# Turning a layer's results on VectorE and through DRAM instead of on TensorE

## The chip, the core and the metric

The kernel runs on one core of a Trainium2 chip. A core has five engines with instruction queues of their own: TensorE (PE, matrix products), VectorE (DVE), ScalarE (ACT), GpSimd (POOL) and SyncE (SP, which here only issues transfers). Each takes its instructions in order, and an instruction that waits holds up all those behind it. Transfers run on the core's 16 DMA engines; they are put on them by SyncE, ScalarE and GpSimd. Matrix products are written to PSUM, everything else works in SBUF.

The metric is the device time of one execution in microseconds, from the first instruction to the last, as the median of several runs. Before the change it is 434.11 us (three runs, 433.49 to 434.98).

## The reference

The computation has two parts. The first is linear attention with a decay, in blocks of 64 positions; its output for 4 sequences of 768 positions becomes 3072 rows (tokens) of 512 numbers:

```python
B, H, S, D = attn_out.shape
x = np.ascontiguousarray(attn_out.transpose(0, 2, 1, 3)).reshape(B * S, H * D)
return _moe_ref(x=x, **moe_kwargs)
```

The second part sends each token to one of eight experts by a hash of its id. An expert is two matrix products with a ReLU between them, and the result is written to the token's own row:

```python
expert_idx = token_ids * np.int64(2654435761) % np.int64(E)
for e in range(E):
    mask = expert_idx == e
    xe = x[mask]
    h = np.maximum(xe @ w1[e], 0.0)
    out[mask] = h @ w2[e]
```

w1 is 512 x 1024 and w2 is 1024 x 512 numbers of four bytes, so each is 2 MB per expert.

## The kernel before, in words

**Stages.** From 0 to about 100 us of the profile runs the attention, in 24 units of 128 positions; its results are stored to a tensor x_pieces in DRAM. Meanwhile the routing is computed: which expert has how many tokens, and lists of row numbers. Then come the experts, one at a time, in eight *windows* (ORDER), each with a fixed number of places for tokens (CAPS, 376 to 432). This document is about the windows.

**A window.** A token's row of x is gathered by GpSimd (gather_window, take) in squares of 32 tokens, turned by VectorE (turn_in), and then lies with features on the partitions and tokens along them. Both layers keep this form: layer one makes hT (1024 features) from xT, layer two makes yT (512 features) from hT. Each layer is done with seven products of quarter size instead of eight (function seven), as in Strassen's method. The sums that this needs are made on VectorE: of the weights (weight_sums, L625), of the tokens (token_sums, L637 and L638) and of the products (L667, L686, L687, L689). The first layer runs seven twice, over two halves of its 1024 features (g = 0 and 1), the second once. In seven, `both` makes products 1 and 2, `others` the products 7, 5, 6, 4 and 3, in that order. The list `todo` holds instructions that `others` hands out between the sums: the weight sums of w2 for this window in the first layer, and in the second layer the weight sums of w1 for the next window and the turn of its x.

**Products and PSUM.** Products 1, 2, 6, 4 and 3 go to the pool psA (4 buffers), 7 and 5 to psC (2 buffers). The pool psB (2 buffers) is free in the windows, except for the results' transposes.

**Getting the results out.** The output needs tokens on the partitions. In the window after the one that made them, tiles_out takes yT in tiles of 128 tokens; rows_out turns each on TensorE with four transposes (L725) into a psB buffer, ScalarE (even tiles, L730) or VectorE (odd tiles, L732) copies it to a tile osb, and GpSimd scatters its rows to the output by their numbers (scatter, L736). Tiles 0 and 1 are done after `both` of the first half, the others after `both` of the second half. w2's columns are ordered in advance so that the copy's rearranging gives the right order of features. The last window has no window after it and calls rows_out itself.

**The order of the work.** It is the order of the program, engine by engine (a manual schedule). Where an instruction stands in the loop over windows therefore decides what it stands behind in its engine's queue. After the code of the first layer the loop issues, on SyncE, the next window's w1 (load_window_w1, L113) and then its w2 (load_window_w2, L119); three buffers of 2 MB hold weights, so a load also waits until its buffer is free. Before each, SyncE reads the expert's number into a register (L123, L127).

Of the kernel before, what the change touches and what calls it, by code (L numbers as in the profile page):

```python
# [7 lines left out]
F32 = mybir.dt.float32  # L8
# [11 lines left out]
CAPS = [376, 384, 392, 392, 400, 408, 416, 432]  # L20
# [5 lines left out]
ORDER = [0, 2, 3, 4, 5, 6, 7, 1]  # L26
SQ = 32
# [4 lines left out]
def kernel(  # L32
# [8 lines left out]
    nc = tc.nc  # L41
    P = 128
# [3 lines left out]
    B, NCH, _, _, D = qkv.shape  # L46
    N, _ = out.shape
    E, _, F = moe_w1.shape
# [3 lines left out]
    NB = P // SQ  # L52
# [10 lines left out]
    DP = D // P  # L63
    FP = F // P
    NT = -(-max(CAPS) // P)
# [3 lines left out]
    def pool(name, bufs, c=ctx, **kw):  # L69
        return c.enter_context(tc.tile_pool(name=name, bufs=bufs, **kw))  # L70
# [18 lines left out]


    x_dram = nc.dram_tensor("x_pieces", ((1 + NC) * DP * P, P), F32)

    order = ExitStack()
    order.enter_context(tc.manual_schedule(engines={
# [136 lines left out]
    idx_all = route.tile([P, NTILE], I32)  # L231
# [289 lines left out]
    def gather_window(e):  # L521


        n = -(-CAPS[e] // SQ)
        xT = xin.tile([P, DP, n * SQ], F32, tag="xT", name=f"xT_{e}")

        g = scratch[:, 0:n * P].rearrange("p (b q) -> p b q", q=P) if e == 0 else xin.tile(
            [P, n, P], F32, tag="g", name=f"g_{e}")

        def gather(b):  # L530
            rows = (1 + (EARLY if e == 0 and b < FIRST // SQ else NC)) * DP * P
            t, k = divmod(b, NB)
            take(g[:, b, :], x_rows[:, e * NT + t, k:k + 1], rows)

        return xT, [lambda b=b: gather(b) for b in range(n)], lambda b0, b1: turn_in(xT, g, b0, b1)
# [68 lines left out]
    mwork = pool("mwork", 2)  # L604
# [12 lines left out]
    def weight_sums(w, name, keep=False):  # L617
        K, M = w.shape[1] // 2, w.shape[2] // 2
        b = [[w[:, j * K:(j + 1) * K, k * M:(k + 1) * M] for k in range(2)] for j in range(2)]
        t = sums.tile([P, 3, K, M], F32, tag=f"t{M}", name=f"{name}_t")  # L620
        t1, t2, t4 = (t[:, i] for i in range(3))
        t3 = sums.tile([P, K, M], F32, tag="t3", name=f"{name}_t3")[:] if keep else b[0][1]
        todo = [(t1, b[0][1], b[0][0]), (t3, b[1][1], b[0][1]), (t2, b[1][1], t1), (t4, b[1][0], t2)]
        return ([None, b[0][0], b[1][0], b[1][1], t4, t1, t2, t3],
                [lambda x=x: nc.vector.tensor_sub(*x) for x in todo])  # L625
# [5 lines left out]
    def token_sums(x, name):  # L631
        a = quarters(x)
        K, M = x.shape[1] // 2, x.shape[2] // 2
        s = sums.tile([P, 3, K, M], F32, tag=f"s{K}", name=f"{name}_s")
        s1, s2, s4 = (s[:, i] for i in range(3))
        s3 = a[1][0]
        todo = [lambda: nc.vector.tensor_add(s1, a[1][0], a[1][1]), lambda: nc.vector.tensor_sub(s2, s1, a[0][0]),  # L637
                lambda: nc.vector.tensor_sub(s3, a[0][0], a[1][0]), lambda: nc.vector.tensor_sub(s4, a[0][1], s2)]  # L638
        return [None, a[0][0], a[0][1], s4, a[1][1], s1, s2, s3], todo

    def flush(todo):
        while todo:
            todo.pop(0)()
# [77 lines left out]
    def rows_out(yT, t, n, idx, apart):  # L721

        ops = psB.tile([P, D], F32, tag="b", name="ops")[0:n]
        for dp in range(DP):
            nc.tensor.transpose(ops[:, dp * P:(dp + 1) * P], yT[:, dp, t * P:t * P + n], ident[:])  # L725
        osb = mwork.tile([P, D], F32, tag="osb", bufs=4, name="osb")[0:n]
        o, i = (osb[:].rearrange("n (a dp d) -> n dp a d", a=DP, d=SQ),
                ops[:].rearrange("n (dp a d) -> n dp a d", a=DP, d=SQ))
        if t % 2 == 0:
            nc.scalar.copy(o, i)  # L730
        else:
            nc.vector.tensor_copy(o, i)  # L732
        scatter(osb, idx, apart)

    def scatter(osb, idx, apart):
        st = nc.gpsimd.indirect_dma_start(  # L736
            out=out[:], out_offset=bass.IndirectOffsetOnAxis(ap=idx, axis=0),
            in_=osb[:], in_offset=None, bounds_check=N - 1, oob_is_err=False)
        if apart:
            tc.declare_no_dep(st.ins, group="out_rows", reason="distinct rows")  # L740
            tc.add_to_no_dep_group("out_rows", st.ins)
# [7 lines left out]
        copy(osb[:].rearrange("n (a dp d) -> n dp a d", a=DP, d=SQ)[:, dps],  # L749
             ps[:].rearrange("n (dp a d) -> n dp a d", a=DP, d=SQ))  # L750

    def tiles_out(e, t0, t1):

        for t in range(t0, min(t1, -(-CAPS[e] // P))):
            n = min(P, CAPS[e] - t * P)
            rows_out(yT, t, n, idx_all[0:n, e * NT + t:e * NT + t + 1], True)

    def squares(e):
        return -(-CAPS[e] // SQ)

    yT = mwork.tile([P, DP, max(map(squares, ORDER)) * SQ], F32, tag="yT", bufs=1, name="yT")
    nc.gpsimd.memset(yT[:, :, CAPS[0]:], 0.0)
    flush(gathers)
    w1_1 = wpool.tile([P, DP, F], F32, tag="w", name="w1_1")
# [3 lines left out]
    for n, e in enumerate(ORDER):  # L768
        then = ORDER[n + 1] if n + 1 < E else None
        hT = sums.tile([P, FP, CAPS[e]], F32, tag="hT", name=f"hT_{e}")  # L770
        b2, todo = weight_sums(w2s[e], f"w2_{e}", keep=then is None)
        if then is not None:
            xT, gathers, turn = gather_window(then)
            xTs[then] = xT[:, :, 0:CAPS[then]]
            flush(gathers)
        if n == 0:

            b1, sums1 = weight_sums(w1s[e], f"w1_{e}", keep=True)
            a1, more = token_sums(xTs[e][:, :, 0:FIRST], f"x_{e}")

            late = [], 3 * [lambda: None] + [lambda: turn0(FIRST // SQ, squares(e))]
            (both0, others0, _, third0), (both1, others1, _, third1) = (
                seven(a1, b1, quarters(hT[:, :, 0:FIRST]), g, True, late[g]) for g in range(2))
            for b in range(NB, FIRST // SQ, NB):
                turn0(b, min(b + NB, FIRST // SQ))

            t1, t3, t2, t4 = sums1
            s1, s2, s3, s4 = more
            flush([s1, s2, s4, s3, t3])
            u1 = [both0()]  # L790
            t1()
            u1.append(both1())
            p3 = third0(), third1()
            t2()
            t4()

            load_window_w2(0, nc.scalar, w2s[0])
            others0(u1[0], p3[0])
            others1(u1[1], p3[1])
            flush(todo)  # L800
            eight(xTs[e][:, :, FIRST:], w1s[e], hT[:, :, FIRST:])
        else:
            past = ORDER[n - 1]
            if then is None:

                nc.gpsimd.drain()
            (both0, others0, *_), (both1, others1, *_) = (seven(a1, b1, quarters(hT[:]), g, True, todo) for g in range(2))
            u1 = both0()
            tiles_out(past, 0, 2)
            others0(u1)  # L810
            u1 = both1()
            tiles_out(past, 2, NT)
            others1(u1)
        if then is None:

            assert CAPS[e] == 3 * P
            a2, sums2 = token_sums(hT[:, :, 0:2 * P], f"h_{e}")
            flush(sums2)
            both, _, last, _ = seven(a2, b2, quarters(yT[:, :, 0:2 * P]), 0, False, [])
            idx = [idx_all[:, e * NT + t:e * NT + t + 1] for t in range(3)]  # L820

            nc.gpsimd.drain()
            last(both(), lambda: rows_out(yT, 0, P, idx[0], True))
            osb = mwork.tile([P, D], F32, tag="osb", bufs=4, name="osb")
            by_rows(hT[:, :, 2 * P:], w2s[e], osb, slice(0, 2))
            rows_out(yT, 1, P, idx[1], True)
            for dp in range(2, DP):
                by_rows(hT[:, :, 2 * P:], w2s[e], osb, slice(dp, dp + 1))
            ntot = nc.values_load(ntot_i[0:1, 0:1], min_val=0, max_val=OCH,
                                  skip_runtime_bounds_check_because="the counts add up to N")  # L830
            scatter(osb, idx[2], True)
            continue
        a2, sums2 = token_sums(hT[:], f"h_{e}")
        if then not in w1s:
            w1s[then] = load_window_w1(then)
        w2s[then] = load_window_w2(then)
        flush(sums2)
        b1, todo = weight_sums(w1s[then], f"w1_{then}")
        todo.insert(2, lambda: turn(0, squares(then)))
        a1, more = token_sums(xTs[then], f"x_{then}")  # L840
        both, others, *_ = seven(a2, b2, quarters(yT[:, :, 0:CAPS[e]]), 0, False, todo)
        others(both())
        flush(todo + more)
# [98 lines left out]
```

## Time and profile before

| | before |
|---|---|
| median of 3 runs | 434.11 us (433.49 to 434.98) |
| span of the profiled execution | 457.4 us |
| mean granted clock of TensorE | 0.959 |
| TensorE matmul busy | 424.8 us, 93% |
| VectorE busy | 309.8 us, 68% |
| ScalarE busy | 78.5 us, 17% |
| GpSimd busy | 191.8 us, 42% |
| transposes of results on TensorE (L725) | 116, of 273 ns each |
| moved by DMA | 78.93 MB |

The profiled execution is longer than the timed ones; shares and orders are read from it, and the time from the runs. In the profile a group of instructions is named by its line, engine, operation, and the tiles that it writes and reads (out<-in). A row of the timeline has start, duration, engine, line, operation and tiles, and in brackets how long the engine stood idle before it and what ended that. A matmul's duration includes the length of TensorE's pipeline, so the rows overlap: what a group takes of the queue is the time from its start to the next one's start. A row of the table of stretches has the stretch, its length, then for each engine its busy time (with the number of records in brackets), the granted clock, the share of the 16 DMA engines, and GB/s. SPq is the queue of SyncE: the row is the issue of a transfer, not its run.

### The profile page before, as it was taken

The numbers are of one execution on the slowest core, as the hardware profiler recorded it, in microseconds if no ns is written. First come the engines' busy times: TensorE is split into PE (matmuls) and PEld (weight loads), VectorE is DVE, ScalarE is ACT, GpSimd is POOL, SyncE is SP. The second block draws the span as 40 slices with busy tenths as digits, with TensorE's granted clock in tenths as the row PEclk, the third lists the DMA queues.
The fourth block names the chain that finished last, engine by engine and source line by source line (L and its number), as shares of the span: only waits on it lengthen the run. The fifth ranks groups of instructions, "written<-read, shape, count | busy, mean of one in ns | idle before, by whom it ended". The sixth has DMA issues, their size and how long they took to land. (4 is left out here: it accounts for less than half of the span.)

```text
span 457.4 us, 8717 instructions
## 1 busy us (share of the span) xinstructions
PE 424.8 (93%) x3474; PEld 402.5 (88%) x3474; DVE 309.8 (68%) x500; ACT 78.5 (17%) x197; POOL 191.8 (42%) x197
## 2 busy tenths in 40 slices
PE   7999999897735999999999999998999999999994
PEld 4888888587724999999999999997999999999993
DVE  5989997577141695868768687864876686858620
ACT  3232333000200012102201310220121012102300
POOL 4557662707774012842673373277027511002101
PEclk9999999889765999999999999999999999999998
DMA  8999999951721542725346063444325260501001
GB/s 317 410 415 417 361 346 358 371 214 40 229 52 44 176 157 80 236 48 218 107 164 242 28 226 93 167 145 139 120 117 180 98 229 27 186 0 47 27 24 47
DMA packets 26026, 78.93 MB, mean 173 GB/s; under 512 B 3461, under 2 KB 3717, under 8 KB 23040
## 3 DMA queue, kind: packets, MB, share of 16 engines
q1 hardware_dynamic: 15920, 56.89, 34.2%
q0 software_dynamic: 5424, 13.05, 8.8%
q10 hardware_dynamic: 4640, 8.42, 5.1%
q8 instruction: 28, 0.46, 0.4%
q14 instruction: 14, 0.11, 0.1%
HBM read 65.50 MB, written 13.11 MB: 172 GB/s over the span
## 5 line engine op out<-in xcount | busy, mean ns | idle before, releaser
L538 POOL DMA_INDIRECT g<-x_pieces,x_rows x91 | 100.4, 1103 | 27.7 <-issue 27.7
L736 POOL DMA_INDIRECT out_dram<-osb,idx_all x30 | 33.2, 1107 | 181.5 <-ACT osb L730 170.6
L657 PE MATMUL p<-hT,w 128*128 128x196 f32 (+6 forms) x368 | 65.4, 338 | 3.9 <-issue 3.9
L657 PEld LDWEIGHTS p<-hT,w 128*128 128x128 f32 x368 | 63.5, 197 | 5.2 <-issue 5.1
L657 PE MATMUL p<-xT,w 128*128 128x196 f32 (+6 forms) x368 | 65.8, 329 | 0.0
L657 PEld LDWEIGHTS p<-xT,w 128*128 128x128 f32 x368 | 60.7, 190 | 0.3 <-issue 0.2
L669 ACT ACTIVATE hT<-hT 128x392 f32<-128x392 f32 (+6 forms) x64 | 32.9, 523 | 116.5 <-DVE hT L667 99.6
L686 DVE TENSOR_TENSOR u<-p,u 128x392 f32<-128x392 f32 (+7 forms) x23 | 13.0, 564 | 52.2 <-PE p L657 41.4
L657 PE MATMUL p<-h_s,w_t 128*128 128x196 f32 (+6 forms) x256 | 44.1, 327 | 2.1 <-issue 2.1
L657 PEld LDWEIGHTS p<-h_s,w_t 128*128 128x128 f32 x256 | 41.8, 190 | 3.3 <-issue 3.3
L657 PE MATMUL p<-x_s,w_t 128*128 128x196 f32 (+6 forms) x256 | 44.6, 327 | 0.0
L667 DVE TENSOR_TENSOR hT<-p,u 128x392 f32<-128x392 f32 (+6 forms) x64 | 35.1, 555 | 10.9 <-ACT u L674 6.9
L657 PEld LDWEIGHTS p<-x_s,w_t 128*128 128x128 f32 x256 | 42.3, 190 | 0.2 <-issue 0.2
L625 DVE TENSOR_TENSOR w_t<-w,w_t 128x1024 f32<-128x1024 f32 x32 | 39.0, 1218 | 0.1
L674 ACT COPY u<-p 128x392 f32<-128x392 f32 (+7 forms) x24 | 11.4, 473 | 158.7 <-PE p L657 130.5
L473 DVE TENSOR_TENSOR sm<-sps,decay 128x512 f32<-128x512 f32 x48 | 30.8, 681 | 5.3 <-remote 3.5
L513 PE MATMUL xps<-sm,qkv 128*64 128x128 f32 x384 | 28.1, 278 | 3.2 <-issue 1.6
L467 PE MATMUL sps<-qkv 64*128 64x128 f32 x384 | 29.9, 296 | 0.4 <-issue 0.2
L625 DVE TENSOR_TENSOR w_t<-w 128x1024 f32<-128x1024 f32 x18 | 21.8, 1217 | 12.0 <-issue 12.0
L667 DVE TENSOR_TENSOR yT<-p,u 128x392 f32<-128x392 f32 (+6 forms) x32 | 17.8, 556 | 17.1 <-PE p L657 10.6
L467 PEld LDWEIGHTS sps<-qkv 64*128 64x128 f32 x384 | 25.2, 198 | 4.8 <-issue 3.4
L479 POOL TENSOR_TENSOR qd<-qkv,q_dec 128x512 f32<-128x512 f32 x16 | 20.4, 1277 | 18.0 <-PE xps L492 11.8
(152 smaller groups left out, 597.9 us busy)
## 6 DMA issues: line engine op xcount, KB each, us to landing
w<-in_moe_w_dram SPq DMA_DIRECT2D x14, 2048.0 KB
qkv<-in_qkv_dram SPq DMA_DIRECT2D x23, 1024.0 KB
x_pieces<-turned ACTq DMA_DIRECT2D x24, 256.0 KB
w<-in_moe_w_dram SPq DMA_DIRECT2D x2, 1024.0 KB
w<-in_moe_w_dram ACTq DMA_DIRECT2D x1, 2048.0 KB
g<-x_pieces,x_rows POOLq DMA_INDIRECT x91
qkv<-in_qkv_dram SPq DMA_DIRECT2D x2, 512.0 KB
out_dram<-osb,idx_all POOLq DMA_INDIRECT x30
```

The costliest lines, as they stand in the source:

```text
L467: nc.tensor.matmul(sps[hd][:, hp, :], kT[half[hd], hp, :], qT[half[hd], hp, :], start=True, stop=True)
L473: nc.vector.tensor_mul(sm[:, hd], sps[hd][:], decay[:, hd])
L479: eng.tensor_tensor(qd[:], qT, q_dec[:], op=OP.mult)
L513: nc.tensor.matmul(xps[half[hd], hp, :], vt[:, 2 * hp + hd, :], sm[:, hd, hp, :], start=(c == 0 and hp == 0), stop=(hp == HP - 1))
L538: nc.gpsimd.indirect_dma_start(out=dst, out_offset=None, in_=x_dram[0:rows, :], in_offset=bass.IndirectOffsetOnAxis(ap=idx, axis=0), bound ...
L625: [lambda x=x: nc.vector.tensor_sub(*x) for x in todo])
L657: nc.tensor.matmul(ps[:, m, :], b[i][:, k, at:at + P], a[i][:, k, :], start=k == 0, stop=k == K - 1)
L667: nc.vector.tensor_add(o, ps[:], u[:])
L669: nc.scalar.activation(o, o, AF.Relu)
L674: nc.scalar.copy(u1[:], product(1)[:])
L686: nc.vector.tensor_add(u2[:], product(6)[:], u1[:])
L736: st = nc.gpsimd.indirect_dma_start(out=out[:], out_offset=bass.IndirectOffsetOnAxis(ap=idx, axis=0), in_=osb[:], in_offset=None, bounds_c ...
```

## The change

The transposes of the results on TensorE are left out. VectorE turns yT in squares of 32 x 32 into a tile o_by, eight squares of tokens at first and then the rest. In o_by the 128 partitions hold, for a square of tokens, four groups of 32 partitions; each group holds the same 32 tokens with another 128 features. SyncE stores each group to a DRAM tensor y_rows, in pieces of 128 numbers (512 bytes), where the four pieces of a token come to lie side by side. Then it reads y_rows back as rows of 512 numbers (2 KB), 128 tokens to a tile osb, and GpSimd scatters these as before. This is to take work off TensorE.

The second part is now handed over before `both` of the second half rather than after it. The last window is as before.

```diff
+    y_dram = nc.dram_tensor("y_rows", (E * NT * P, D), F32)
...
-    def tiles_out(e, t0, t1):
-
-        for t in range(t0, min(t1, -(-CAPS[e] // P))):
-            n = min(P, CAPS[e] - t * P)
-            rows_out(yT, t, n, idx_all[0:n, e * NT + t:e * NT + t + 1], True)
+    def turn_out(e, b0, b1):
+
+
+        nc.vector.transpose(o_by[:, b0:b1, :].rearrange("p b (dp d) -> p b dp d", d=SQ),
+                            yT[:, :, b0 * SQ:b1 * SQ].rearrange("p dp (b r) -> p b dp r", r=SQ))
+        rows = y_dram[e * NT * P:(e + 1) * NT * P, :]
+        for a in range(DP):
+            nc.sync.dma_start(rows[b0 * SQ:b1 * SQ, a * P:(a + 1) * P].rearrange("(b r) q -> r b q", r=SQ),
+                              o_by[a * SQ:(a + 1) * SQ, b0:b1, :])
+        for t in range(b0 // NB, -(-b1 // NB)):
+            n = min(P, b1 * SQ - t * P)
+            osb = mwork.tile([P, D], F32, tag="osb", bufs=4, name="osb")
+            nc.sync.dma_start(osb[0:n], rows[t * P:t * P + n, :])
+            n = min(n, CAPS[e] - t * P)
+            scatter(osb[0:n], idx_all[0:n, e * NT + t:e * NT + t + 1], True)
...
             u1 = both0()
-            tiles_out(past, 0, 2)
+            turn_out(past, 0, 2 * NB)
             others0(u1)
-            u1 = both1()
-            tiles_out(past, 2, NT)
-            others1(u1)
+            turn_out(past, 2 * NB, squares(past))
+            others1(both1())
```

P is 128, D is 512, SQ is 32, and DP, NB and NT are 4; `past` is the window before.

More of the change, by code (lines that the diff above doesn't have):

```diff
@@ L737, in scatter @@
             out=out[:], out_offset=bass.IndirectOffsetOnAxis(ap=idx, axis=0),
-            in_=osb[:], in_offset=None, bounds_check=N - 1, oob_is_err=False)
+            in_=osb, in_offset=None, bounds_check=N - 1, oob_is_err=False)
         if apart:
@@ L761 @@
     yT = mwork.tile([P, DP, max(map(squares, ORDER)) * SQ], F32, tag="yT", bufs=1, name="yT")
+    o_by = mwork.tile([P, max(map(squares, ORDER)), P], F32, tag="o_by", bufs=1, name="o_by")
     nc.gpsimd.memset(yT[:, :, CAPS[0]:], 0.0)
```

## The prediction

> **What bounds the kernel now.** I read the page first, then the table of stretches for one expert, then TensorE's timeline around the code that changes, then VectorE's and SyncE's for the same stretch. The page's first part, and two stretches cut at the edges of one expert's two layers (window 3, 392 tokens; first layer from 203.53, second from 223.86):
>
> ```profile
> PE 424.8 (93%) x3474; PEld 402.5 (88%) x3474; DVE 309.8 (68%) x500; ACT 78.5 (17%) x197; POOL 191.8 (42%) x197
> ...
> 203.53:223.86 20.33, 20.33 (x130) 20.19 (x129) 15.23 (x25) 4.99 (x10) 6.04 (x6) 1.00 0.41 144
> 223.86:242.43 18.57, 18.57 (x113) 18.57 (x113) 14.19 (x17) 1.52 (x3) 14.36 (x12) 1.00 0.50 156
> ```
>
> In both stretches TensorE is busy for all of the time, at full granted clock; VectorE is busy for 15.23 of 20.33 us. So TensorE's own work sets the time of an expert, and from 147 us on nearly everything is experts. Both layers hold 112 of TensorE's records for products of the same size; the first layer is 20.33 - 18.57 = 1.76 us longer, and the timeline shows by what:
>
> ```profile
> 203.53 2.82 PE L657 MATMUL p<-xT,w 128*128 128x196 f32 x16
> 206.19 1.04 PE L725 MATMUL ops<-ident,yT 128*128 128x128 f32 x8
> 207.06 1.49 PE L657 MATMUL p<-xT,w 128*128 128x196 f32 x8
> ...
> 216.35 1.04 PE L725 MATMUL ops<-ident,yT 128*128 128x128 f32 x8
> 217.22 1.49 PE L657 MATMUL p<-xT,w 128*128 128x196 f32 x8
> ...
> 223.86 8.12 PE L657 MATMUL p<-hT,w 128*128 128x196 f32 x48
> ```
>
> Eight transposes take the queue from 206.19 to 207.06, and eight more from 216.35 to 217.22: 0.87 us each time, 0.109 us a transpose, with no gap around them.
>
> **What the Trainium skill says.** "TensorE: Matmul & The Clock Gate", Part 4, gives a transpose in a kernel's context as about 275 ns. The trace has 273 ns as its length, but 109 ns from start to start, and that is what leaving one out is worth in a full queue. "VectorE: DVE Perf Modes", The three transpose paths, says VectorE turns 32x32 blocks only; so the rest of the move has to be done by DMA, which is the trip through DRAM. "DMA: Bandwidth & Descriptors", Anatomy of one DMA, puts the fixed part of a DMA at about 2.0 us, most of it the receipt of the write, and says that a wait for a semaphore is made by the sequencer that issues; Two DMAs through the same engine are not ordered says that a read of what an earlier DMA wrote needs such a wait. Before, no DMA of SyncE waits for another to land in this way, so the trace neither confirms nor denies it; the nearest row is the last x_pieces store, issued at 99.4 us, whose bytes move from 100.3 to 101.0 with a few packets until 102.5: 1.6 to 3.1 us.
>
> **Part by part.** *TensorE.* tiles_out goes, and with it 12 transposes for window 0 and 16 for each of the six other windows: 108 of 116 (the last window's 8 stay, in rows_out). 108 x 0.109 = 11.7 us off the bounding engine. ScalarE loses 13 copies of 0.57 us; it is busy 17%, so nothing comes of that.
>
> *VectorE.* Out go two copies per window (0.69 and 0.67 us); in come two transposes. By the rows for this kind (512 columns 0.67 us, 1664 columns 1.904 us: 1.07 ns a column above the first) 1024 columns cost 1.22 us and 640 cost 0.81: +0.67 us per window on an engine with 5 us free in that layer. The first one must not hold up what follows it:
>
> ```profile
> 206.46 0.57 DVE L667 TENSOR_TENSOR hT<-p,u 128x392 f32<-128x392 f32 x1
> 207.26 0.69 DVE L732 COPY osb<-ops 128x512 f32<-128x512 f32 x1 [0.24 <-PE ops L725]
> 207.87 1.22 DVE L625 TENSOR_TENSOR w_t<-w 128x1024 f32<-128x1024 f32 x1
> 209.12 1.23 DVE L625 TENSOR_TENSOR w<-w 128x1024 f32<-128x1024 f32 x1
> 211.25 0.57 DVE L686 TENSOR_TENSOR u<-p,u 128x392 f32<-128x392 f32 x1 [0.90 <-PE p L657]
> ```
>
> It needs no wait for TensorE: start 207.0, end 208.2, two subtractions, so the add of L686 is ready at 210.7. Its product ends at 211.25 - 0.87 = 210.4. VectorE is 0.3 us late, once, while four psA buffers stand between the engines; and the later half has 2.58 us of idle time before its own L686. No cost. The second transpose stands between the two halves: the chain of adds, 5.4 us before, ends at 216.1, the transpose at 216.9.
>
> *SyncE: the new wait.* Each call of turn_out puts four stores of y_rows on SyncE's queue and then the loads of osb, which wait for the stores to land. Behind them in the same queue stands the load of the next window's w1. Today:
>
> ```profile
> 203.73 0.38 SPq L113 DMA_DIRECT2D w<-in_moe_w_dram  x1
> 224.06 0.38 SPq L119 DMA_DIRECT2D w<-in_moe_w_dram  x1
> ```
>
> L113 (w1) goes out 0.2 us after the first layer starts, L119 (w2) as the second starts. Afterwards w1 goes out only behind the second turn_out. I count from the start of TensorE's second layer, which moves to 223.86 - 1.74 = 222.1. Second transpose done: 216.9, or -5.2. Four stores at 0.38 us (the L113 row): the last begins at -4.0. Receipt 1.6 to 3.1 us; I take 2.3, the skill's 2.0 and a little for 512-byte pieces: -1.7. Two loads: -0.9. Reading the expert's number into a register and issuing took 0.8 us at 79.9 to 80.7: w1 goes out at -0.1; with the short receipt at -0.8; with the long one and 0.5 us a store, +1.2. So it leaves some 18 us later than now.
>
> How long does it take? In one-microsecond stretches of the DMA view from 203.7, the queue of SyncE moves 0, 0.11, 0.28, 0.40, 0.41, 0.43, 0.42 MB and ends in the eighth: 7.1 us alone. The w2 load of 224.06, beside gathers, takes 9.2. In its new place w1 lies beside the end of the osb loads, two scatters (about 0.3 MB) and the first gathers, so near 0.5 MB at 0.42 MB/us more: 8.5. It lands at +8.4 (bounds +6.3 and +10.5).
>
> When is it needed?
>
> ```profile
> 230.40 0.57 DVE L667 TENSOR_TENSOR yT<-p,u 128x392 f32<-128x392 f32 x1 [1.88 <-PE p L657]
> 230.88 1.22 DVE L625 TENSOR_TENSOR w_t<-w 128x1024 f32<-128x1024 f32 x1
> ...
> 237.33 0.57 DVE L686 TENSOR_TENSOR u<-p,u 128x392 f32<-128x392 f32 x1 [2.15 <-issue]
> ...
> 242.63 0.57 DVE L667 TENSOR_TENSOR yT<-p,u 128x392 f32<-128x392 f32 x1 [0.33 <-PE p L657]
> 244.21 0.57 DVE L638 TENSOR_TENSOR xT<-xT 128x400 f32<-128x400 f32 x1
> ```
>
> The subtraction at 230.88 is the first reader: +7.0. VectorE will stand there 1.4 us, and everything queued on it behind: the second subtraction, the turn of the next x, the add of L686. That lateness is absorbed in order: 2.15 us of idle time before 237.33, 0.33 before 242.63, and 0.4 more, since TensorE's third product of the next layer, at 242.43 + 2.7 = 245.1 without transposes, needs the sum at 244.21, done at 244.7. So w1 may land until 7.0 + 2.9 = +9.9 before TensorE waits. Expected +8.4: no stall. At the worst bound, +10.5: 0.6 us in each of six windows (the last has no w1 to load), 3.6 us. I enter 0.1 us a window, 0.6 in all, for a margin of only 1.5 us.
>
> *Other work, at nothing.* w2 queues behind w1, lands near +15, and is first read 4.4 us into the next layer, at about +23. The scatters move by the round trip, some 5 us, and the gathers queued behind them; but a window's gathers are issued one window before the turn that reads them (first at 222.0, turn at 271.7). The added 11.6 MB of DRAM traffic falls first on a stretch (213 to 221) where the DMA share is 0.00. The four osb buffers were scattered one window earlier.
>
> Sum: 434.1 - 11.7 + 0.6 = **423.0 us**.
>
> **Rivals.** (1) *w1 comes late by a little*: both unknowns fall near their upper ends, w1 out at +1.2, and w2 right behind plus gathers make it 9.5 us, so it lands at +10.7 and TensorE waits 0.8 us in six windows: 422.4 + 4.8 = 427.2. For it: the margin is 1.5 us and two receipts and a shared DMA lie in it; against it: the DMA is idle when the stores go. (2) *w1 replaces the transposes as the bound*: the 512-byte stores take about 2 us more than my upper end (out at +3.2, landing at +12.7): 2.8 us x 6 = 16.8, so 422.4 + 16.8 = 439.2, slower. For it: no store in 512-byte pieces from 32 partitions is in the trace; against it: the four stores of a call together are only 0.33 MB. (3) *VectorE becomes the bound* through its added 0.67 us and a transpose in the middle of a chain: if all of it, and 0.3 us for each first transpose, showed, 7 x 0.97 = 6.8: 429.2. Against it: 5 us idle in the layer, and the copy that waited for TensorE is gone.
>
> **How the numbers follow.** Forecast 0.62, rival 1 0.17, rival 2 0.14, rival 3 0.07. The range must leave out rival 2 (0.14) and may lose a little of the tails of the rest: 421.0 (every transpose at its start-to-start time, and 1.4 us for waits on ScalarE's and VectorE's copies that go too) to 431.0. Faster by over 0.3%, below 432.8: 0.62 + 0.17 + 0.07, less 0.06 for the gap between rivals 1 and 2: 0.80. Within 0.3%: 0.05. Slower: 0.15.
>
> **What would show it.** Right: L725 with 8 records only; a first layer as long as the second; L113 on SyncE's queue at 0 to +1 of the second layer; VectorE idle for 1 to 2 us before the first subtraction of w1, put down to the load; TensorE without gaps. Wrong: gaps in TensorE before the third product of a first layer, or osb loads that start over 4 us after the last store; or a VectorE idle time over 2.9 us before w1's subtraction, which would carry over to TensorE and turn the sign if it passed 4.8.

## The result and the profile after

The changed kernel takes **422.9 us** (four runs, 421.81 to 423.05) beside 434.35 us for the kernel before (four runs, 433.49 to 434.98). The ratio is 0.9732, with a 95% interval of 0.9708 to 0.9756: 2.7% faster. The forecast was 423.0. Here and below a ratio uses the undisturbed executions alone, on both sides (all of them here and in e1 to e4, but only 3 of 22 and 3 of 7 of the changed kernel's on the two other chips), while a median is over all runs.

The lines below are from three parts of the page after: busy times, and two of the transfers' rows (tiles, queue, count, KB each, median us from issue to landing). Line numbers have moved, those of the products and sums by three: L660 for L657, L628 for L625, L689 for L686, L641 for L638.

```profile
PE 402.2 (96%) x3366; PEld 386.4 (92%) x3366; DVE 314.4 (75%) x501; ACT 72.0 (17%) x183; POOL 191.7 (46%) x197
...
osb<-y_rows SPq DMA_DIRECT2D x21, 256.0 KB, 2.8
y_rows<-o_by SPq DMA_DIRECT2D x28, 128.0 KB, 2.5
```

TensorE has 108 records fewer and is busy for 22.6 us less. Not all of that is the transposes: the profile before was taken in an execution of 457 us in which TensorE also stood and ran at a lower granted clock (0.83, then 0.60) for no shown cause, chiefly between 105 and 147 us. So where the gain came from is read from the windows alone, and from an experiment (e3 below). The stretches, cut again at the edges of layers (first layer, second layer, first layer of the next window):

```profile
181.36:199.93 18.57, 18.57 (x113) 18.57 (x113) 15.61 (x24) 4.04 (x8) 5.08 (x5) 1.00 0.42 117
199.93:218.50 18.57, 18.57 (x113) 18.57 (x113) 13.56 (x17) 1.52 (x3) 12.94 (x12) 1.00 0.82 289
218.50:237.52 19.02, 19.02 (x115) 18.91 (x113) 16.18 (x25) 4.09 (x8) 5.43 (x5) 1.00 0.44 118
```

The first layer is now exactly as long as the second, 18.57 us for 392 tokens (before 20.33 and 18.57); the third stretch has wider products, for 400 tokens. TensorE is busy throughout at full clock. The price shows in the last two columns: the second layer's DMA share went from 0.50 to 0.82, because the load of the next w1 has moved into it from the first layer.

TensorE's timeline of the same window: no transposes, and no idle time in brackets.

```profile
181.36 4.14 PE L660 MATMUL p<-xT,w 128*128 128x196 f32 x24
...
199.93 8.12 PE L660 MATMUL p<-hT,w 128*128 128x196 f32 x48
...
218.50 4.29 PE L660 MATMUL p<-xT,w 128*128 128x200 f32 x24
...
228.05 4.22 PE L660 MATMUL p<-xT,w 128*128 128x200 f32 x24
```

The first product group of the next window (218.50) takes 4.29 us where the same group of its second half takes 4.22. The 0.07 us lie in one matmul at 221.21, the first that reads a sum which VectorE ended at 221.12, right behind VectorE's longest wait. They are the only delay in the windows. SyncE's queue:

```profile
194.51 1.97 SPq L762 DMA_DIRECT2D y_rows<-o_by  x4
198.69 0.81 SPq L767 DMA_DIRECT2D osb<-y_rows  x2
200.34 0.41 SPq L116 DMA_DIRECT2D w<-in_moe_w_dram  x1
201.58 0.41 SPq L122 DMA_DIRECT2D w<-in_moe_w_dram  x1
```

Four stores, then 2.2 us of waiting for their receipt, the notice that they have landed (196.48 to 198.69), two loads, and only then w1 (L116), 0.4 us after the second layer's start; w2 follows at once. In the six windows w1 leaves at +0.25, +0.4, +0.2, -0.3, +1.4 and -0.7 us, on average +0.2. And VectorE, which needs it:

```profile
205.51 0.57 DVE L670 TENSOR_TENSOR yT<-p,u 128x392 f32<-128x392 f32 x1 [0.96 <-PE p L660]
209.89 1.23 DVE L628 TENSOR_TENSOR w_t<-w 128x1024 f32<-128x1024 f32 x1 [3.82 <-DMA w<-in_moe_w_dram]
...
214.13 0.53 DVE L689 TENSOR_TENSOR u<-p,u 128x392 f32<-128x392 f32 x1
...
218.98 0.56 DVE L670 TENSOR_TENSOR yT<-p,u 128x392 f32<-128x392 f32 x1
...
220.55 0.57 DVE L641 TENSOR_TENSOR xT<-xT 128x400 f32<-128x400 f32 x1
```

VectorE stands for 3.82 us until w1 is there, at +9.96 (counted, as in the prediction, from the second layer's start), and behind that not one idle time in brackets is left: it reaches L641 at 220.55 with all slack used up. TensorE's third product of the next layer, due 2.7 us after 218.50, reads what L641 writes until 221.1. Over all windows, from VectorE's table of waits after 147 us (what waited, on what: us in total, times, longest):

```profile
DVE w_t L628 <- DMA w<-in_moe_w_dram: 18.5, 6, 3.8
```

So the change swapped 108 transposes for 18.5 us of waiting on another engine, of which TensorE sees 0.07.

### The profile page after: what moved, and what is told of

It reads as the page before. It is cut to its first block, busy times and chain, and to the rows that moved or that the text cites. A ratio compares the mean times of both kernels' runs of the same rounds, so it can differ in the third digit from the quotient of the medians.

```text
span 420.9 us, 8620 instructions
## 1 busy us (share of the span) xinstructions
PE 402.2 (96%) x3366; PEld 386.4 (92%) x3366; DVE 314.4 (75%) x501; ACT 72.0 (17%) x183; POOL 191.7 (46%) x197
## 5 line engine op out<-in xcount | busy, mean ns | idle before, releaser
L541 POOL DMA_INDIRECT g<-x_pieces,x_rows x91 | 98.7, 1084 | 27.7 <-issue 27.1
L739 POOL DMA_INDIRECT out_dram<-osb,idx_all x30 | 34.4, 1147 | 148.8 <-DMA osb<-y_rows 124.5
L660 PE MATMUL p<-hT,w 128*128 128x196 f32 (+6 forms) x368 | 64.0, 334 | 4.0 <-DVE hT L641 2.2
L660 PEld LDWEIGHTS p<-hT,w 128*128 128x128 f32 x368 | 62.5, 194 | 4.4 <-DVE hT L641 2.5
L660 PE MATMUL p<-xT,w 128*128 128x196 f32 (+6 forms) x368 | 63.5, 329 | 0.0
L660 PEld LDWEIGHTS p<-xT,w 128*128 128x128 f32 x368 | 61.2, 190 | 0.3 <-issue 0.2
L660 PE MATMUL p<-x_s,w_t 128*128 128x196 f32 (+6 forms) x256 | 44.4, 327 | 0.0
L628 DVE TENSOR_TENSOR w_t<-w 128x1024 f32<-128x1024 f32 x18 | 21.6, 1207 | 29.0 <-DMA w<-in_moe_w_dram 29.0
L660 PE MATMUL p<-h_s,w_t 128*128 128x196 f32 (+6 forms) x256 | 43.0, 326 | 0.0
L660 PEld LDWEIGHTS p<-x_s,w_t 128*128 128x128 f32 x256 | 42.2, 190 | 0.0
L660 PEld LDWEIGHTS p<-h_s,w_t 128*128 128x128 f32 x256 | 41.9, 190 | 0.0
L628 DVE TENSOR_TENSOR w_t<-w,w_t 128x1024 f32<-128x1024 f32 x32 | 38.9, 1217 | 0.1
L689 DVE TENSOR_TENSOR u<-p,u 128x392 f32<-128x392 f32 (+7 forms) x23 | 12.9, 560 | 25.9 <-PE p L660 25.9
L470 PE MATMUL sps<-qkv 64*128 64x128 f32 x384 | 28.5, 290 | 0.6 <-DMA qkv<-in_qkv_dram 0.6
L482 POOL TENSOR_TENSOR qd<-qkv,q_dec 128x512 f32<-128x512 f32 x16 | 20.4, 1275 | 18.0 <-PE xps L495 10.7
L470 PEld LDWEIGHTS sps<-qkv 64*128 64x128 f32 x384 | 24.1, 193 | 4.8 <-issue 2.7
L516 PE MATMUL xps<-sm,qkv 128*64 128x128 f32 x384 | 26.3, 275 | 1.3 <-DVE sm L476 1.1
L660 PE MATMUL p<-x_s,w 128*128 128x196 f32 (+6 forms) x128 | 24.6, 340 | 2.7 <-issue 2.7
```

The lines of the kernel that those rows point to most:

```text
L470: nc.tensor.matmul(sps[hd][:, hp, :], kT[half[hd], hp, :], qT[half[hd], hp, :], start=True, stop=True)
L482: eng.tensor_tensor(qd[:], qT, q_dec[:], op=OP.mult)
L516: nc.tensor.matmul(xps[half[hd], hp, :], vt[:, 2 * hp + hd, :], sm[:, hd, hp, :], start=(c == 0 and hp == 0), stop=(hp == HP - 1))
L541: nc.gpsimd.indirect_dma_start(out=dst, out_offset=None, in_=x_dram[0:rows, :], in_offset=bass.IndirectOffsetOnAxis(ap=idx, axis=0), bound ...
L660: nc.tensor.matmul(ps[:, m, :], b[i][:, k, at:at + P], a[i][:, k, :], start=k == 0, stop=k == K - 1)
L689: nc.vector.tensor_add(u2[:], product(6)[:], u1[:])
```

## The experiments

The theory: the gain is the transposes' queue time alone (108 x 0.109 us), everything added is hidden, and the delay of w1 is hidden up to a limit of about +10 us for its landing. The rivals: that the delay of w1 or the trip already costs something, so that the transposes are worth more than was seen; or that the gain has another source. e1 to e4 ran side by side on one chip, where the kernel before took 433.41 us, 0.9 less than above. The changed kernel itself was not among them, so ratios are compared, and stretches of the profiles.

**e1: w1 ahead of the trip.** The load moves ahead of the first layer's code, before `both` of the first half.

```diff
+            if then is not None:
+                w1s[then] = load_window_w1(then)
             u1 = both0()
             turn_out(past, 0, 2 * NB)
...
-        if then not in w1s:
-            w1s[then] = load_window_w1(then)
```

> The changed kernel with one line moved: the load of the next window's w1 is issued on SyncE ahead of the first turn_out of a window, not behind the second. My theory (TensorE's own work is the bound, and the late w1 is absorbed by VectorE's idle time): VectorE's waits for w1, 18.5 us in all in the changed kernel, go to under 1 us, TensorE's layers keep their length, and the time stays at 422.9 us within 0.5. Rival (the late w1 takes back a part of the gain): 1.5 us or more faster than the changed kernel, 421.4 or less.

Measured: 422.16 us (421.97 to 422.63), ratio 0.9741 (0.9713 to 0.9768). VectorE's timeline at the same place as above, in e1:

```profile
204.69 0.57 DVE L670 TENSOR_TENSOR yT<-p,u 128x392 f32<-128x392 f32 x1 [0.96 <-PE p L660]
205.17 1.22 DVE L628 TENSOR_TENSOR w_t<-w 128x1024 f32<-128x1024 f32 x1
...
212.58 0.57 DVE L689 TENSOR_TENSOR u<-p,u 128x392 f32<-128x392 f32 x1 [3.11 <-PE p L660]
```

The wait for w1 is gone in every window, and VectorE idles for 3.11 us at the next place instead, for TensorE. The median is 0.7 us lower, and the kernel before was 0.9 lower here too; the ratios are the same within their intervals. So the 18.5 us of waiting cost nothing that can be measured.

**e2: no trip.** The results are scattered straight from o_by: the stores of y_rows and the loads of osb are left out, so that other numbers go to the output's rows, in the same amount.

```diff
-        for a in range(DP):
-            nc.sync.dma_start(rows[...].rearrange("(b r) q -> r b q", r=SQ), o_by[a * SQ:(a + 1) * SQ, b0:b1, :])
         for t in range(b0 // NB, -(-b1 // NB)):
...
-            nc.sync.dma_start(osb[0:n], rows[t * P:t * P + n, :])
-            scatter(osb[0:n], ...)
+            scatter(o_by[0:n, at:at + NB, :].rearrange("p b q -> p (b q)"), ...)
```

> The changed kernel without the trip through DRAM: no stores to y_rows and no loads from it; GpSimd scatters rows straight from o_by. The seven windows' rows then hold the right tokens' slots with other numbers in them, and the last tile of a window takes its rows from the last four squares. All else as in the changed kernel, VectorE's transposes too. My theory: 422.4 to 422.9 us, as the trip is wholly hidden; w1 goes out within 0.3 us of the start of a first layer again. Rival (11.6 MB of DRAM traffic, or the waits on SyncE, cost something): 421.4 or less.

Measured: 421.47 us (420.13 to 422.45), ratio 0.9718 (0.969 to 0.9746). The median alone decides nothing: it lies under the forecast and just above the rival's line, with the kernel before 0.9 us lower too. But the intervals of e1, e2 and the changed kernel overlap, and from the first layer of the second window to the second layer of the last, the stretch called *the seven windows* below, the changed kernel's profile has 249.36 us, e1's 249.30 and e2's 249.29. The 11.9 MB of added traffic and SyncE's wait (32.3 us in 26 waits) cost nothing that can be measured.

**e3: the kernel before, with the trip added.** The transposes on TensorE and the copies stay; VectorE's transposes, stores and loads are added, into a tile that nobody reads.

```diff
             tiles_out(past, 0, 2)
+            turn_out(past, 0, 2 * NB)
             others0(u1)
+            turn_out(past, 2 * NB, squares(past))
             u1 = both1()
             tiles_out(past, 2, NT)
             others1(u1)
```

> The kernel before, with its transposes on TensorE, copies and scatters, and the new work as well: VectorE's transposes into o_by, the stores to y_rows and the loads back, into a tile that nobody reads. The output is not touched by the added work. My theory: the added work costs nothing, so 434.4 us within 0.7; w1 goes out late, but the first layer is 1.74 us longer than in the changed kernel, so that VectorE waits for it under 2 us each time. Rival (the added work costs a few us, and the transposes were worth more than 11.7): 437 or more. Second rival (the gain came from the order of the two halves or the copies that went): 432 or less.

Measured: 433.43 us (431.41 to 436.61), ratio 1.0007 (0.9983 to 1.003). In e3's profile the transposes are back in TensorE's queue, and VectorE waits for w1 here too:

```profile
182.87 2.82 PE L658 MATMUL p<-xT,w 128*128 128x196 f32 x16
185.53 1.04 PE L726 MATMUL ops<-ident,yT 128*128 128x128 f32 x8
186.40 1.49 PE L658 MATMUL p<-xT,w 128*128 128x196 f32 x8
```

```profile
DVE w_t L626 <- DMA w<-in_moe_w_dram: 10.5, 5, 3.2
```

The waits, 3.2 us at most, are longer than the 2 us I had expected; TensorE again shows none. The seven windows of the changed kernel and of e3, each as one stretch:

```profile
144.21:393.57 249.36, 249.36 (x1458) 249.25 (x1457) 197.47 (x265) 38.24 (x74) 100.02 (x90) 1.00 0.57 186
144.41:405.53 261.12, 261.12 (x1566) 260.31 (x1565) 205.95 (x278) 44.90 (x88) 102.21 (x92) 1.00 0.56 180
```

TensorE has no gap in either, at full clock. The difference is 11.76 us for 108 records, and 108 x 0.109 is 11.77. With all that the change adds, and with what it takes away still there, the time is that of the kernel before. The two kernels also differ in the copies and in where the scatters take their rows from, but in neither does TensorE wait for these. So the whole gain is the transposes on TensorE.

**e4: w1 later still.** Two small transfers from DRAM to DRAM are put ahead of the load of w1, the second waiting for the first.

```diff
+            nc.sync.dma_start(hop[2 * n], y_dram[past * NT * P:past * NT * P + 32, 0:P])
+            nc.sync.dma_start(hop[2 * n + 1], hop[2 * n])
             w1s[then] = load_window_w1(then)
```

> The changed kernel with two small transfers from DRAM to DRAM (16 KB) put on SyncE's queue ahead of the load of the next w1; the second waits for the first, so w1 goes out about 3.3 us later. In the changed kernel w1's first subtraction starts 9.0 to 10.3 us after the second layer's start; my theory puts the limit at about +9.9 to +10.3, so TensorE then stands about 2.7 us in each of six windows, ahead of the third product of the first layers: 435 to 441 us. Rival (there is more slack than I counted, or w1 is not on TensorE's path at all): under 426 us.

Measured: 434.31 us (432.48 to 438.81), ratio 1.0026 (0.9996 to 1.0057). VectorE's and TensorE's waits in e4, one line from each table:

```profile
DVE w_t L629 <- DMA w<-in_moe_w_dram: 34.9, 6, 8.3
```

```profile
PE p L661 <- DVE xT L642: 9.3, 5, 3.9
```

w1 leaves at +3.4, +2.4, +3.9, +2.6, +3.2 and +2.1 us, on average 2.7 us later than in the changed kernel, and TensorE stands 3.20, 0.88, 3.95, 0.38, 0.94 and 0 us behind it. Past the limit the lateness of w1 turns into a stop of TensorE one for one: in the first of these windows w1 is there 2.3 us later than in the second (+13.33 and +11.04), and the stop is 2.3 us longer. The first of the stops, on VectorE and then on TensorE:

```profile
175.06 1.23 DVE L629 TENSOR_TENSOR w_t<-w 128x1024 f32<-128x1024 f32 x1 [6.83 <-DMA w<-in_moe_w_dram]
```

```profile
180.31 2.82 PE L661 MATMUL p<-xT,w 128*128 128x196 f32 x16
186.32 2.38 PE L661 MATMUL p<-xT,w 128*128 128x196 f32 x8 [3.20 <-DVE xT L642]
188.49 3.76 PE L661 MATMUL p<-x_s,w_t 128*128 128x196 f32 x16
```

The second layer starts at 161.73, so w1 is there at +13.33, and TensorE stops before the third product of the next first layer, where the prediction had put it. 13.33 - 3.20 gives the limit: +10.1 us. The same difference in the next four is 10.2, 10.7, 10.9 and 11.1: the limit comes later as the windows get wider. The gaps add up to 9.35 us, but the seven windows take 263.48, 14.1 us more than after. Three quarters of the rest lie right behind the two long gaps: in the last fence eight products take 2.17 us of the queue instead of 1.33 and the next sixteen 3.60 instead of 2.65, 1.8 us in all, and after the gap of 3.95 us it is 1.8 us again. My 435 to 441 was just missed on the low side. 2.7 us of delay on a transfer that VectorE reads first, and TensorE only in the next layer, take away the whole gain.

**Other chips.** Two more kernels undo a part of the change: e5 leaves the second part of the results to TensorE and ScalarE/VectorE as before, and e6 puts the second part behind `both` again, as in the order of the kernel before.

```diff
+            u1 = both1()
+            tiles_out(past, 2, NT)
+            others1(u1)
-            turn_out(past, 2 * NB, squares(past))
-            others1(both1())
```

```diff
+            u1 = both1()
             turn_out(past, 2 * NB, squares(past))
-            others1(both1())
+            others1(u1)
```

They ran with the changed kernel and e1 on a chip on which the kernel before took 474.74 us, and again, without e1, on one on which it took 462.49. The expectations, in the order after, e1, e5, e6:

> The changed kernel once more, beside the next three on one chip, so that differences of one us can be read. Every theory: its ratio to the kernel before is 0.973 to 0.975.

> w1 first, once more, beside the changed kernel on the same chip. My theory: the same within 0.5 us, since the changed kernel's TensorE has no gaps but 0.07 us in one window. Rival (late w1 costs something that the one profile doesn't show): 1.0 us or more faster than the changed kernel.

> The changed kernel with a part of the old way back: tiles 0 and 1 of a window take the trip through DRAM, the tiles from 2 on are turned on TensorE and copied, at their old place. 52 of the 108 transposes are back (4 for window 0, 8 for each of the six others). My theory (each transpose costs 0.109 us of TensorE's queue and nothing else): 52 x 0.109 = 5.7 us slower than the changed kernel, and VectorE hardly waits for w1, which goes out after the first part's loads. Rival (what matters is the copies, the psB buffers or the order): under 3 or over 8 us.

> The changed kernel with the second turn_out after both of the second half, where the old tiles_out stood, and not before it. VectorE's second transpose, and with it w1, comes some 0.8 us later. The changed kernel's w1 subtraction starts at +9.0 to +10.3 us of the second layer and the limit is at about +10, so my theory gives TensorE gaps of 0 to 0.8 us in six windows: 1 to 3 us slower than the changed kernel. Rival (there is slack left): the same within 0.5 us.

And for the other chip, in the order after, e5, e6:

> The changed kernel beside the next two on one chip; the last set ran on a chip where TensorE stood for long stretches in every kernel. Where the kernel before takes about 434 us, every theory has 422 to 423 us.

> 52 of the 108 transposes back on TensorE, the tiles from 2 on without the trip. My theory where the kernel before takes about 434 us: 5.7 us slower than the changed kernel, about 428.5. Rival (copies, psB buffers or order matter): under 3 or over 8 us.

> The second turn_out after both of the second half. My theory where the kernel before takes about 434 us: w1 goes out some 0.8 us later, TensorE gaps of 0 to 0.8 us in six windows ahead of the third product of the first layer, 1 to 3 us slower than the changed kernel. Rival (there is slack left): the same within 0.5 us.

Measured (median in us, range; ratio to the kernel before with its interval):

```
        chip with before at 474.74                     chip with before at 462.49
after   473.02 (462.39-486.2)   0.9789 (0.9713-0.9865)   465.6  (454.68-473.3)   0.9899 (0.9838-0.9959)
e1      470.87 (461.71-482.4)   0.9749 (0.965-0.9848)    -
e5      462.6  (458.83-464.0)   0.9735 (0.967-0.9799)    454.99 (450.04-459.21)  0.987  (0.9821-0.9919)
e6      478.04 (465.7-485.08)   0.988  (0.9836-0.9925)   465.99 (461.52-471.68)  1.0085 (1.0049-1.0122)
```

The ratios give the changed kernel a gain of 1 to 2% here, but by the medians of all runs it is 0.4% faster on the one chip and 0.7% slower on the other. So a gain like the first one isn't shown on these chips. e5, which was to be 5.7 us slower than the changed kernel where the kernel before takes about 434, is 10 us faster by its medians. In the profiles from these chips most of the extra time comes after 80 us, and some 20 us or more of it lie ahead of the windows: the seven windows start at 164 to 172 us, beside 143 to 144 in the changed kernel's first profile and in e1 to e4. What happens in the windows shows in the second run of the changed kernel; TensorE's and then VectorE's timeline from 327 to 344 us:

```profile
331.40 0.34 PE L660 MATMUL p<-xT,w 128*128 128x208 f32 x1 [0.27 <-issue]
332.81 1.32 PE L660 MATMUL p<-xT,w 128*128 128x208 f32 x4 [1.08 <-issue]
334.94 1.22 PE L660 MATMUL p<-xT,w 128*128 128x208 f32 x3 [0.81 <-issue]
...
340.28 3.14 PE L660 MATMUL p<-xT,w 128*128 128x208 f32 x8 [2.72 <-DVE xT L641]
```

```profile
327.81 0.58 DVE L689 TENSOR_TENSOR u<-p,u 128x408 f32<-128x408 f32 x1 [2.90 <-PE p L660]
...
336.39 0.58 DVE L670 TENSOR_TENSOR yT<-p,u 128x408 f32<-128x408 f32 x1 [5.14 <-remote]
```

"issue" and "remote" are the profile's words where it shows no cause. Between 330 and 337 us VectorE stands for 5.14 us and TensorE goes on by a few matmuls at a time; then VectorE is behind, and TensorE waits 2.72 us for its sum. TensorE's waits for VectorE's sums were 13.9 and 16.7 us in the two profiles of e6, 7.6 and 14.9 in those of the changed kernel, 4.0 and 0 in those of e5. One account is that the stretches use up the slack on VectorE that hides the lateness of w1: it fits e5, whose w1 leaves 9 us before the second layer, and e6, whose w1 comes latest. Against it stands e1: its w1 leaves with the first layer, and its profile there has 10.3 us of the same waits. The profiled executions are also unlike in length (450 to 482 us). So the account isn't shown, and the order of e5 and e6 isn't explained.

One thing can be read there exactly. In e5's second profile the seven windows have no gap:

```profile
166.20:421.35 255.15, 255.15 (x1511) 254.32 (x1510) 195.59 (x264) 41.55 (x81) 102.27 (x92) 1.00 0.53 167
```

That is 5.79 us more than the changed kernel's 249.36, for 52 transposes put back: 0.111 us each. The gain grows with the number of transposes taken out.

**The kernel before on another chip**, to learn if the gaps of its first profile (457 us beside timed runs of 434) belonged to that one execution:

> The kernel before, profiled once more, because in its first profile TensorE stood for some 20 us between 105 and 147 us and 3 us near 315 with nothing that the profile shows as the cause, which other kernels with the same code there don't show. My theory: that was of one profiled execution, and this one has a span near 433 us and no such gaps. Rival: the kernel before always loses this time in its first window, and a part of the gain lies there.

Measured: 471.97 us, span 470.3. Two of its rows, from TensorE's and from VectorE's waits after 150 us:

```profile
PE p L657 <- issue: 5.8, 10, 1.4
```

```profile
DVE yT L667 <- remote: 18.3, 4, 7.9
```

My expectation of about 433 missed: the stretches occur in the kernel before as well, on a third chip, and a second execution of it there took 471.64. They aren't made by the change. What makes them stays open; the profiles show nothing that both engines wait for.

## Why the prediction was right

- **TensorE bounds; 108 x 0.109 = 11.7 us go.** Shown by e3, 11.76 us, and by e5, 0.111 us each. "TensorE: Matmul & The Clock Gate", Part 4, of the Trainium skill gives about 275 ns for a transpose of 128x128 bf16 in a kernel's context; the fp32 ones here were 273 ns long. An estimate at that figure, 108 x 0.275 = 30 us, would have been far off. ScalarE lost 14 copies and VectorE 13, not the other way round as the prediction had it; nothing came of it.
- **VectorE's transposes: 1.22 and 0.81 us, at no cost.** Measured 1.23 and 0.84. The first chain was to be 0.3 us late once; it shows no idle time at all, and TensorE none.
- **SyncE's wait.** The prediction counted 2.3 us (1.6 to 3.1) from the start of the last store to the first load; for the second part of a window it was 2.0 to 4.4 us, 3.0 on average, so this term was too small. The section of the Trainium skill that the prediction took 2.0 us from ("DMA: Bandwidth & Descriptors", Anatomy of one DMA) is on transfers issued by GpSimd; SyncE's 128 KB stores landed 2.5 us after their issue in the median. w1 was to leave at -0.1 (-0.8 to +1.2): +0.2 on average, -0.7 to +1.4. One wait of 4.4 us was over the 4 us named as a sign of being wrong, and TensorE shows no gap behind it.
- **w1 lands at +8.4 (6.3 to 10.5).** This term was too small: over six windows the load lands and the first subtraction starts at +9.0 to +10.3, on average +9.5. The load took 8.7 to 9.9 us, on average 9.3, not 8.5. It ran beside w2 right behind it and the gathers, with the DMA engines busy for 0.82 of the layer; that this made it longer isn't shown. VectorE also reached the subtraction earlier than +7.0, at +6.1 in the window shown. Together: 3.1 us of waiting per window where I had 1.4. For the same reason the sign that I named, over 2.9 us of waiting, was too strict: three of the six waits are over it, and from +6.1 to the limit it is 3.8 us.
- **The limit of +9.9.** Right for the window that it was counted in, and the forecast hung on it: 0.07 us of delay at +9.96, and +10.1 to +10.2 from e4. In a wider window w1 came at +10.3 with no delay; e4 puts the limit there at +11.1. Against the limits of e4, w1 came 0.2 us to at least 1.8 us early, 1.2 on average, where the margin was to be 1.5. That is in part luck: w1 was 1.1 us later than forecast, and the limits of most windows were later too. Of the 0.1 us a window that I entered for the thin margin, 0.07 was seen, once.
- **Scatters, gathers, w2, traffic at nothing.** e2 and e3: nothing measurable. GpSimd waits 124.5 us for the loads of osb before its scatters, all hidden.
- **The rivals.** Rival 2, w1 as the bound, was missed by little: with w1 2.7 us later, at +2.9 on average, e4 lost the whole gain. Its time stays under the 439.2 of the rival, which had w1 at +3.2, as TensorE's stops are 1.6 us per window (9.35 / 6) and not 2.8. Rival 1 had w1 leave 1 us later than it did on average. Rival 3 had nothing for it: VectorE went from 68 to 75%, and TensorE waited for it for 0.07 us in all.

The sum: 434.35 - 422.9 is 11.5 us, where 11.7 - 0.6 was written. That the time itself was met within 0.1 us is luck too, since the kernel before was 0.24 us slower in the four runs than in the three that the prediction started from. The prediction says nothing of chips on which the engines stand for other reasons, and there no such gain is shown.

## What to carry to other kernels

On the bounding engine price an instruction by the time from its start to the next one's start, not by its length: a transpose here was 0.273 us long and was worth 0.109. When a transfer that waits for another's receipt is put into a queue, ask at once what stands behind it in that queue: here the wait cost nothing itself, but it made a 2 MB load leave 18.6 us later (from +0.2 of the first layer to +0.2 of the second), and the number that decided was how late that load may land before the chain of readers reaches the bounding engine. If such a load doesn't depend on the waiting one, issue it first, as e1 does: same time, and 3 us of slack per window back.

## What the runs showed of the hardware

In e4 a stop of TensorE of 3 to 4 us cost more than its length. These are the stretches around the first gap (columns as in the tables of stretches above; the granted clock is the third number from the end):

```profile
183.10:186.32 3.22, 0.02 (x1) 0.00 (x1) 3.19 (x7) 0.00 (x0) 0.58 (x1) 1.00 0.18 38
186.32:188.49 2.17, 2.17 (x8) 2.17 (x9) 2.17 (x4) 0.53 (x1) 0.00 (x0) 0.65 0.00 0
188.49:192.00 3.51, 3.51 (x17) 3.51 (x17) 2.21 (x2) 0.00 (x0) 0.00 (x0) 0.73 0.61 149
192.00:195.00 3.00, 3.00 (x20) 3.00 (x19) 2.65 (x5) 0.53 (x1) 0.00 (x0) 1.00 0.48 165
```

After 3.2 us without work the clock is 0.65 and then 0.73, and full again from 192: 5.7 us at about 0.7, so 1.8 us lost on top of 3.2. After the gap of 3.95 us it was 0.55 for the first 2.35 us. The gap of 0.88 us was followed by eight products of 128x200 within 1.62 us, which elsewhere take 1.52. The Trainium skill says in "TensorE: Matmul & The Clock Gate", Part 1, that the clock falls to half after an idle window of some 3.4 us; here a stop of 3.2 us was enough for a mean of 0.65. In this run the waits of up to a microsecond were paid about once, and the two of over three were paid one and a half times.

Unexpected too was that one and the same kernel takes 433 us on one chip and 462 to 475 on others. The profiles there have stretches of several microseconds in which VectorE stands and TensorE goes on by single matmuls, with no cause shown.
